# Splitting the first-layer weights of two experts in the second group instead of the first, from pieces loaded a second time

## The chip, the cores and the metric

The kernel runs on one core of one Trainium2 chip. Time is device time in microseconds (us). The kernel before was run three times: 985.46, 986.72 and 987.31, median 986.72. Beside these there is one profiled execution, of 984.69 us; every time that is quoted from a profile is counted from the start of its span, in which the instructions lie (982.9 us).

## What is computed

Two blocks in a row. The first is a recurrent attention over 4 batches, 8 heads, 768 positions and head size 48:

```python
state = alpha[:, :, t, :, None] * state + k[:, :, t] (outer) v[:, :, t]
y[:, :, t] = q[:, :, t] @ state
```

Its output is laid out as x with 3072 rows and 384 columns. The second block adds up four experts, each a pair of matrix products:

```python
p = domain_probs / (domain_probs.sum(-1, keepdims=True) + 1e-09)
for e in range(4):
    h = np.maximum(x @ w1[e], 0.0)          # 384 -> 1024
    out += p[:, e:e + 1] * (h @ w2[e])      # 1024 -> 384
```

All inputs and the output are 32-bit floats.

## The kernel before

The 3072 rows are 24 units of 128 rows, one for each batch and each block of 128 positions. The units stand in seven groups: group 0 has two units, groups 1 to 5 have four, group 6 has two. For each group and expert the kernel runs a first layer, `up` (L922), in eight chunks of 128 hidden columns, and a second layer, `down` (L982), which adds up each unit's 384 output columns over the chunks. The experts are taken in the order 0, 1, 2, 3 in even groups and 3, 2, 1, 0 in odd ones (`expert`, L196), so that the last expert of a group is the first of the next and its weights stay where they are. In group 1 the order is therefore 3, 2, 1, 0. Below, up(1,2) is the first layer of group 1 with the expert at place 2 of its order, which is expert 1.

The attention of a group's units runs beside the layers of the group ahead: `deal` (L1069) lays out by hand-written costs and due times when each step of a unit's attention is put into the program, and `advance` (L1125) puts in what is due after each chunk or step. All engines' queues are in the order in which the program was written (manual_schedule, L1131), and each engine works its queue in that order: PE (TensorE) for the products, ACT (ScalarE) and DVE (VectorE) for everything that reads PSUM and for the attention's elementwise work, POOL (GpSimd) for the stores and some multiplications, SP (SyncE) for the loads.

**Weights.** Group 0 multiplies with the weights as they are (L951 and L1023, tile raw). From group 1 on each weight is used as two parts, a rounded top and the rest, and each product is made of three (`PRODUCTS`, L101). `split_piece` (L240) makes the parts of a piece, a quarter of one expert's layer (128 partitions by 768 numbers): ACT copies the piece into the rounded type (L250), DVE subtracts it from the piece (L252), and POOL stores both parts, 768 KB, to the buffer `kept` in DRAM (L253). `background` (L255) carries the splits on, one step of each open split and one new one per call. In group 0 all four experts' first-layer pieces are split, in group 1 the second-layer pieces (and the last expert's first two of them at the end of group 0).

`load_piece` (L213) loads. A raw piece is 384 KB, from the weights themselves (L232 for the first layer, L236 for the second); a split one is 768 KB from kept (L225). In up(g,e) the next expert's first-layer pieces are loaded at the end of chunks 1, 3, 5 and 7 (L971), into one of four buffers, when PE has read the piece that was there.

**The pool raw** has twelve buffers of one piece each, which are handed out in turn. Raw pieces take them, and from the end of group 1 on the in-order attention (units from the eleventh on) keeps eight for good: two for the loads of q by fours (L184), one zeroed block (L553), one for quads (L611), two for AT and QT (L481), and two for the last group's x (L657).

The rows that the prediction follows, by line: in the attention of a unit, DVE transposes alpha, k and q (L702; L488 in the in-order form); ACT copies half of q (qb, L756) and of k (L774) level by level, and DVE multiplies both with the decays (L763, L775); PE makes the scores (sc L782, far L838), DVE takes them under masks (L792), ACT copies them into lat (L851, L855); PE makes yps (L877) and sps (L904), ACT and DVE turn yps into the two parts of x (L889, L890), DVE updates the state (L909 to L912). In the layers: PE one (L951, L957), ACT relu (hT L953, L959), DVE the rest of hT (L979), PE ops (L1023), and ACT or DVE add ops up into acc (L1047, L1049). ops and one share four PSUM buffers.

Of the kernel before, what the change touches and what calls it, by code (L numbers as in the profile page):

```python
# [20 lines left out]
def kernel(  # L21
# [134 lines left out]
    def load(u, names):  # L156
        if u >= len(units):
            return
        cb, b = units[u]
        for nm in names:  # L160
            src = srcs[nm][b, :, cb * P:(cb + 1) * P, :].rearrange("h s d -> s h d")
            if u == in_fours and nm == "q":
                nc.gpsimd.memset(row_a, 1.0)
            if u == in_runs and nm != "v":
                nc.gpsimd.memset(runs_of[nm][:, :, RUN - HD // 4:], 0.0)
            for g in range(P // QUAD if u >= in_runs and nm != "v" else 0):
                i, tail = divmod(g, 2)
                off, n = (QUAD, RUN - HD // 4) if tail else (0, RUN)
                runs = srcs[nm][b].rearrange("(a i) s d -> i a (s d)", i=2)[
                    i, :, cb * P * D:(cb + 1) * P * D].rearrange("a (t n) -> t a n", t=QUAD)  # L170
                nc.sync.dma_start(out=runs_of[nm][QUAD * g:QUAD * (g + 1), :, :n],
                                  in_=runs[:, :, off:off + n])
            if u >= in_runs and nm == "a":
                continue
            if u < in_fours or nm != "q":
                nc.sync.dma_start(out=raw(u, nm)[:, :, :D], in_=src)
                continue
            by_four = lambda t: t[b, :, cb * P:(cb + 1) * P].rearrange("h (t f) d -> t h (f d)", f=FOUR)
            if u == in_fours:
                four_tiles.extend(whole_raw().rearrange("p (h f d) -> p h f d", f=FOUR, d=D) for _ in range(2))  # L180
            fours[u] = four_tiles
            for i, t in enumerate(fours[u]):
                for j in range(FOUR):
                    nc.sync.dma_start(out=t[j::FOUR].rearrange("p h f d -> p h (f d)"),  # L184
                                      in_=by_four(q)[:, H // 2 * i:H // 2 * (i + 1)])
            for j in range(FOUR - 1):
                nc.sync.dma_start(out=row_a[j::FOUR].rearrange("p h f d -> p h (f d)")[:, :, D * j:],
                                  in_=by_four(alpha)[:, :, D * (j + 1):])
# [13 lines left out]
        return kept[l][expert(gi, e) * NQ + c]  # L202

    AHEAD = 4
    RAW = 3 * NQ

    def parts_of(l):
        return wts.tile([P, 2, KC * QF], F32R, name=f"w{l + 1}", bufs=AHEAD if l == 0 else NQ)
# [4 lines left out]
    def load_piece(l, i, beside=False, held=None):  # L213
        if i >= E * NQ * LAST:
            return
        gi, k = divmod(i, E * NQ)
        at, c = divmod(k, NQ)
        e = expert(gi, at)
        if at == 0 and gi > 0:
            if held is not None:  # L220
                wt[l][i] = held
            return
        if gi > l:
            w = wt[l][i] = parts_of(l)
            nc.sync.dma_start(out=w.bitcast(F32), in_=stored(l, i))  # L225
            return
        if l == 1 and gi == 0 and not beside:
            return
        w = work.tile([P, KC * QF], F32, name="raw", bufs=RAW)
        wt[l][i] = w  # L230
        if l == 0:
            nc.sync.dma_start(  # L232
                out=w.rearrange("p (c f) -> p c f", f=QF),
                in_=moe_w1[e].rearrange("(c p) f -> p c f", p=P)[:, :, c * QF:(c + 1) * QF])
        else:
            nc.sync.dma_start(  # L236
                out=w.rearrange("p (c d) -> p c d", d=DM),
                in_=moe_w2[e].rearrange("(c p) d -> p c d", p=P)[:, c * FPQ:(c + 1) * FPQ])

    def split_piece(l, i):  # L240
        gi, k = divmod(i, E * NQ)
        whole = wt[l][i]
        w = parts_of(l)
        if l == 1:
            wt[l][i] = w
        elif k >= (E - 1) * NQ:
            wt[l][i + NQ] = w
        top, rest = (w[:, part] for part in range(2))

        nc.scalar.copy(out=top, in_=whole)  # L250
        yield
        nc.vector.tensor_sub(rest, whole, top.bitcast(F32))  # L252
        nc.gpsimd.dma_start(out=stored(l, i), in_=w.bitcast(F32))  # L253
# [212 lines left out]
        load(2, "v")  # L466
        yield

    def whole_raw():
        return work.tile([P, KC * QF], F32, name="raw", bufs=RAW)  # L470

    def in_order(u):
        cb, b = units[u]
        k = u - in_fours
# [1 line left out]
        if k < 2:  # L476
            AT_of.append(work.tile([P, NP, P], F32, name="AT"))
            QT_of.append(work.tile([P, NP, P], F32, name="QT"))
        elif k == 2:
            for tiles in (AT_of, QT_of):  # L480
                tiles.append(whole_raw()[:, :NP * P].rearrange("p (a n) -> p a n", n=P))  # L481
        AT, QT = AT_of[k % 3], QT_of[k % 3]
        rv = values[u % 2]

# [65 lines left out]
            next_k(li)  # L550
            yield
        if k == 0:
            fifth = whole_raw()[:, :NP * P].rearrange("p (a i n) -> p a i n", i=2, n=HALF)  # L553
            nc.gpsimd.memset(fifth, 0.0)
            free.append(fifth)
        for li in range(2, 6):
# [51 lines left out]
        if keep:  # L608
            next_k(6)
            if not quads:  # L610
                quads.append(whole_raw()[:, :NP * P])  # L611
# [24 lines left out]
        def tail():  # L636
# [17 lines left out]
            if slot == 0 and gi < LAST:  # L654
                xTs[gi] = work.tile([P, 2, KC, NT], F32R, name="xT", bufs=2)
            elif slot == 0:
                xTs[gi] = [work.tile([P, KC * QF], F32R, name="raw", bufs=RAW) for _ in range(2)]  # L657
# [32 lines left out]
    def attention(u):  # L690
# [172 lines left out]
        def result():  # L863
            yps = ps.tile([P, KC, P], F32, name="yps", tag="w")
            strips = [[] for _ in range(P // QUAD)]
            for c in range(KC):
                for j, strip in enumerate(strips):
                    p, part = divmod(len(strips) * c + j, 3)
                    terms = [(flat_st[:, p, QUAD * part:QUAD * (part + 1)], QT[:, p, :])] if cb > 0 else []
                    for i in range(2):  # L870
                        if part != 2 * (1 - i):
                            at = VD * (2 * p + i) + QUAD * part - D * i
                            terms.append((flat_v[:, at:at + QUAD], lat[:, 2 * p + i, :]))
                    strip += [(c, n == 0, n == len(terms) - 1, *term) for n, term in enumerate(terms)]
            for turn in zip(*strips):
                for j, (c, begins, ends, lhsT, rhs) in enumerate(turn):
                    nc.tensor.matmul(yps[QUAD * j:QUAD * (j + 1), c, :], lhsT=lhsT, rhs=rhs,  # L877
                                     start=begins, stop=ends)
            gi, slot = place[cb, b]
            cols = slice(slot * P, (slot + 1) * P)  # L880
            if gi == 0:
                nc.scalar.copy(out=xTs[gi][:, 0, :, cols], in_=yps)
                return
            if slot == 0 and gi < LAST:
                xTs[gi] = work.tile([P, 2, KC, NT], F32R, name="xT", bufs=2)
            elif slot == 0:
                xTs[gi] = [work.tile([P, KC * QF], F32R, name="raw", bufs=RAW) for _ in range(2)]
            top, low = (x_part(gi, part)[:, :, cols] for part in range(2))
            nc.scalar.copy(out=top, in_=yps)  # L889
            nc.vector.tensor_sub(low, yps, top.bitcast(F32))  # L890
# [31 lines left out]
    def up(gi, e, fc, slots=None):  # L922
# [59 lines left out]
    def down(gi, e, slots):  # L982
# [234 lines left out]
```

## Time and profile before

| | us |
|---|---|
| three runs, median | 986.72 |
| the profiled execution | 984.69 |
| its span | 982.9 |
| PE busy | 960.5 (98%) |
| DVE busy | 602.2 (61%) |
| ACT busy | 382.7 (39%) |
| POOL busy | 107.1 (11%) |
| group 0, from the first product of up(0,0) to the last of down(0,3) | 21.8 to 151.6 |
| group 1: up(1,1), down(1,1) | 194.1 to 214.0, to 235.1 |
| up(1,2), down(1,2) | to 254.3, to 275.4 |
| up(1,3), down(1,3) | to 296.6, to 318.3 |

The clock that PE was granted is full (0.998). The DMA engines moved 188.56 MB, 29.49 MB of it on the queue of POOL, the rest almost all on that of SP.

How to read the views that follow. A line of the timeline has the start and length in us, the engine, the line of the kernel, the operation, what it writes <- what it reads, the shapes and how many instructions were merged; in square brackets stands how long the engine was idle before, and what ended the idle time. SPq lines are SP issuing a DMA, not the transfer. PEld is PE's loading of weights, which runs beside its products.

### The profile page before, as it was taken

To read this page: it belongs to the slowest core of one execution; us is meant where nothing else is said; L and a number is where in the kernel's file an instruction comes from. 1 tells how busy PE (TensorE), PEld (TensorE's weight loads), DVE (VectorE), ACT (ScalarE), POOL (GpSimd) and SP (SyncE) were. 2 spreads that over 40 slices of the span, in tenths; PEclk is the share of its full clock that TensorE was granted. 3 is DMA by queue.
4 is the path that set the end of the run, shared out by engine and by line. 5 is a ranking of instruction groups with operands and counts; after the bars stand their busy time and mean duration, and the time that the engine had idled before them with its cause. 6 is when DMAs were issued, how large, how long until landed. Compare 5 with 4: busy or idle time off the path is not lost.

```text
span 982.9 us, 20423 instructions
## 1 busy us (share of the span) xinstructions
PE 960.5 (98%) x8168; PEld 859.1 (87%) x8168; DVE 602.2 (61%) x1208; ACT 382.7 (39%) x834; POOL 107.1 (11%) x137
## 2 busy tenths in 40 slices
PE   8998899999999999999999999999999999999998
PEld 7776677988989889899899899898898999999997
DVE  4788878576788958668558577568677312222222
ACT  4767655463543542432433423434334122111111
POOL 2000001000212210110210110210120000000000
PEclk9999999999999999999999999999999999999999
DMA  9798977485964877864667884669782006060601
GB/s 196 261 298 223 302 219 253 157 260 170 313 214 141 251 229 224 303 221 114 194 209 238 284 240 117 186 196 270 243 213 78 34 1 257 1 254 3 242 31 33
DMA packets 171490, 188.56 MB, mean 192 GB/s; under 512 B 80588, under 2 KB 151116, under 8 KB 171396
## 3 DMA queue, kind: packets, MB, share of 16 engines
q1 hardware_dynamic: 164932, 157.41, 53.3%
q0 software_dynamic: 6016, 29.49, 7.9%
q8 instruction: 64, 1.05, 0.4%
q10 hardware_dynamic: 448, 0.36, 0.1%
q14 instruction: 30, 0.25, 0.1%
HBM read 154.71 MB, written 32.51 MB: 190 GB/s over the span
## 4 chain that ended last, share of the span: by engine, by line
PE 81%; DVE 9%; ACT 4%; DMA 3%; issue 2%; SPq 0%; DVEq 0%; POOL 0%; ACTq 0%; POOLq 0%
PE ops L1023 38%; PE one L957 31%; PE sc L578 3%; PE yps L650 2%; ACT qb L756 2%; DVE w L252 1%; PE sc L782 1%; DVE hT L979 1%; PE yps L877 1%; PE one L951 1%; DMA raw<-in_moe_w_dram 1%; DVE near L792 1%; DMA w<-kept 1%; PE tp L283 1%; PE far L586 1%
## 5 line engine op out<-in xcount | busy, mean ns | idle before, releaser
L1023 PE MATMUL ops<-w,hT 128*128 128x384 f32 x2112 | 377.9, 338 | 2.4 <-DVE hT L979 2.3
L1023 PEld LDWEIGHTS ops<-w,hT 128*128 128x128 f32 x2112 | 365.2, 188 | 8.2 <-DVE hT L979 4.1
L957 PE MATMUL one<-xT,w 128*128 128x512 f32 x1440 | 333.2, 390 | 0.1
L957 PEld LDWEIGHTS one<-xT,w 128*128 128x128 f32 x1440 | 269.4, 188 | 56.7 <-DVE hT L979 1.0
L959 ACT ACTIVATE hT<-one 128x512 fp32r<-128x512 f32 (+1 forms) x192 | 108.0, 563 | 315.6 <-PE one L957 315.0
L979 DVE SCALAR_TENSOR_TENSOR hT<-one,hT 128x512 fp32r<-128x512 f32 (+1 forms) x192 | 121.0, 641 | 106.7 <-ACT hT L959 106.6
L1049 DVE SCALAR_TENSOR_TENSOR acc<-ops,p_all,acc 128x384 f32<-128x384 f32 x66 | 38.7, 610 | 87.0 <-PE ops L1023 86.9
L756 ACT COPY qb<-QT 64x256 f32<-64x256 f32 x126 | 51.5, 409 | 33.3 <-DVE QT L763 17.9
L531 DVE TENSOR_TENSOR QT<-QT,AT 128x256 f32<-128x256 f32 x70 | 33.1, 472 | 50.4 <-ACT qb L525 40.0
L492 POOL TENSOR_TENSOR ra<-ra 128x384 f32<-128x384 f32 x28 | 28.7, 1026 | 298.8 <-DMA ra<-in_alpha_dram 297.7
L951 PE MATMUL one<-xT,raw 128*128 128x256 f32 (+1 forms) x240 | 44.9, 340 | 0.4 <-ACT xT L453 0.4
L1058 POOL DMA_DIRECT2D out_dram<-acc x22 | 12.0, 548 | 305.3 <-DVE acc L1049 304.4
L1023 PE MATMUL ops<-raw,hT 128*128 128x384 f32 x128 | 44.9, 493 | 0.0
L253 POOL DMA_DIRECT2D kept<-w x32 | 17.2, 539 | 247.6 <-DVE w L252 120.1
L951 PEld LDWEIGHTS one<-xT,raw 128*128 128x128 f32 x240 | 38.0, 191 | 5.2 <-ACT xT L453 0.6
L763 DVE TENSOR_TENSOR QT<-QT,AT 128x256 f32<-128x256 f32 x60 | 25.3, 421 | 26.2 <-ACT qb L756 25.8
L494 POOL TENSOR_TENSOR raw<-raw,ra 128x576 f32<-128x576 f32 x28 | 40.6, 1470 | 1.1
L957 PE MATMUL one<-raw,w 128*128 128x256 f32 x288 | 35.2, 283 | 0.0
L957 PEld LDWEIGHTS one<-raw,w 128*128 128x128 f32 x288 | 35.1, 192 | 0.0
L1023 PEld LDWEIGHTS ops<-raw,hT 128*128 128x128 f32 x128 | 23.1, 190 | 13.4 <-issue 0.6
L525 ACT COPY qb<-QT 64x256 f32<-64x256 f32 x80 | 32.1, 402 | 7.0 <-DVE QT L531 3.5
L792 DVE COPY_PREDICATED near<-masks,sc 128x256 f32<-128x256 uint8 x54 | 28.8, 533 | 7.2 <-PE sc L782 6.2
(163 smaller groups left out, 957.9 us busy)
## 6 DMA issues: line engine op xcount, KB each, us to landing
w<-kept SPq DMA_DIRECT2D x108, 768.0 KB, 6.1
kept<-w POOLq DMA_DIRECT2D x32, 768.0 KB, 6.8
raw<-in_moe_w_dram SPq DMA_DIRECT2D x44, 384.0 KB, 7.1
raw<-in_q_dram SPq DMA_DIRECT2D x112, 96.0 KB, 2.8
rv<-in_v_dram SPq DMA_DIRECT2D x24, 192.0 KB, 3.8
rk<-in_k_dram SPq DMA_DIRECT2D x22, 192.0 KB, 2.9
out_dram<-acc POOLq DMA_DIRECT2D x22, 192.0 KB, 2.3
sa<-in_alpha_dram SPq DMA_DIRECT2D x44, 88.0 KB, 3.7
```

Of the source, the lines that this page charges most:

```text
L494: nc.gpsimd.tensor_mul(t[:, :, 1:], t[:, :, 1:], row_a[:, H // 2 * i:H // 2 * (i + 1)])
L525: nc.scalar.copy(out=qbs[li][rows, :, i, :].rearrange("p a (b r) -> p a b r", r=m), in_=qv[rows])
L531: nc.vector.tensor_mul(qv, qv, spread(dv[:, :, :, 0], m))
L578: nc.tensor.matmul(banks[li // 2 - 1][HALF * s:HALF * (s + 1), li % 2, 2 * p:2 * p + 2, :], lhsT=KTs[li][:, p, HALF * s:HALF * (s + 1)], r ...
L756: nc.scalar.copy(out=qb[rows, :, i, :].rearrange("p a (b r) -> p a b r", r=m), in_=qv[rows])
L792: nc.vector.copy_predicated(near.rearrange("p a (b two r) -> p a b two r", two=2, r=m)[:, :, :, 1, :], mk.unsqueeze(1).broadcast_to([P, H, ...
L951: nc.tensor.matmul(one, lhsT=w[:, kc], rhs=xTs[gi][:, 0, kc, lo:hi], start=(kc == 0), stop=(kc == KC - 1))
L957: nc.tensor.matmul(one, lhsT=w[:, of_w, kc], rhs=x_part(gi, of_x)[:, kc, :n], start=k == 0, stop=k == len(turns) - 1)
L959: nc.scalar.activation(out=parts[0], in_=one, func=ACT.Relu)
L979: nc.vector.scalar_tensor_tensor(out=low, in0=x, scalar=0.0, in1=top.bitcast(F32), op0=ALU.max, op1=ALU.subtract)
L1023: nc.tensor.matmul(sums[slot], lhsT=h, rhs=w, start=(n == begins[slot]), stop=(n == ends[slot]))
L1049: nc.vector.scalar_tensor_tensor(out=acc, in0=part, scalar=scale, in1=acc, op0=ALU.mult, op1=ALU.add)
```

## The change

The first-layer pieces of experts 0 and 1 (places 0 and 1, `LATE = 2`) are not split in group 0 any more. In group 1 those experts stand at places 3 and 2. Where the kernel before loads their two parts from kept in up(1,1) and up(1,2), the changed one loads the raw piece again into the pool raw; and down(1,1) and down(1,2) then hand four splits each to `background`, which in a second layer of group 1 is called at each twelfth of its 96 steps. There each split takes a buffer of w1 and stores its parts to kept as before. The four w1 splits of the first expert at down(0,0) and the four of the second (two in down, two in up(0,1)) are gone. The pool raw becomes twelve tiles with names of their own, that a list hands out in turn; what the attention keeps is taken out of the list.

```diff
-    RAW = 3 * NQ
+    def raw_tile(i, dtype=F32):
+        return work.tile([P, KC * QF], dtype, name=f"raw{i}", bufs=1)
+
+    raws = deque((i, raw_tile(i)) for i in range(3 * NQ))
+
+    def whole_raw(keep=False):
+        if keep:
+            return raws.popleft()[1]
+        raws.rotate(-1)
+        return raws[-1][1]
...
-        if gi > l:
+        late_split = l == 0 and gi == 1 and e < LATE
+        if gi > l and not late_split:
             w = wt[l][i] = parts_of(l)
             nc.sync.dma_start(out=w.bitcast(F32), in_=stored(l, i))
             return
         if l == 1 and gi == 0 and not beside:
             return
-        w = work.tile([P, KC * QF], F32, name="raw", bufs=RAW)
+        w = whole_raw()
...
+    LATE = 2
+
     def split_piece(l, i):
         gi, k = divmod(i, E * NQ)
         whole = wt[l][i]
         w = parts_of(l)
-        if l == 1:
+        if gi == 1:
             wt[l][i] = w
...
-        if gi == 0 and e > 0 and fc in SPLIT_AT:
+        if gi == 0 and e >= LATE and fc in SPLIT_AT:
             making.append(split_piece(0, e * NQ + SPLIT_AT[fc]))
...
-        if gi == 0 and e < E - 1 and slots[0] == (e == 0):
+        if gi == 0 and LATE <= e + 1 < E and slots[0] == (e == 0):
             making.extend(split_piece(0, first + NQ + k) for k in range(2))
...
         while fresh(gi) and (making or splitting):
             background()
+        if gi == 1 and E - LATE <= e + 1 < E:
+            making.extend(split_piece(0, first + NQ + k) for k in range(NQ))
...
-            if n == FCH // 2 and ahead:
-                making.extend(split_piece(0, k) for k in range(NQ))
```

At the places that keep a buffer, `whole_raw()` becomes `whole_raw(keep=True)`, and the last group's x takes `raw_tile(raws.popleft()[0], F32R)`.

More of the change, by code (lines that the diff above doesn't have):

```diff
@@ L179, in load @@
             if u == in_fours:
-                four_tiles.extend(whole_raw().rearrange("p (h f d) -> p h f d", f=FOUR, d=D) for _ in range(2))
+                four_tiles.extend(whole_raw(keep=True).rearrange("p (h f d) -> p h f d", f=FOUR, d=D) for _ in range(2))
             fours[u] = four_tiles
@@ L467, in rest_of_first @@
         yield
-    def whole_raw():
-        return work.tile([P, KC * QF], F32, name="raw", bufs=RAW)
     def in_order(u):
@@ L480, in in_order @@
             for tiles in (AT_of, QT_of):
-                tiles.append(whole_raw()[:, :NP * P].rearrange("p (a n) -> p a n", n=P))
+                tiles.append(whole_raw(keep=True)[:, :NP * P].rearrange("p (a n) -> p a n", n=P))
         AT, QT = AT_of[k % 3], QT_of[k % 3]
@@ L552, in in_order @@
         if k == 0:
-            fifth = whole_raw()[:, :NP * P].rearrange("p (a i n) -> p a i n", i=2, n=HALF)
+            fifth = whole_raw(keep=True)[:, :NP * P].rearrange("p (a i n) -> p a i n", i=2, n=HALF)
             nc.gpsimd.memset(fifth, 0.0)
@@ L610, in in_order @@
             if not quads:
-                quads.append(whole_raw()[:, :NP * P])
+                quads.append(whole_raw(keep=True)[:, :NP * P])
             by_quad = quads[0].rearrange("x (t a c) -> x t a c", a=NP, c=QUAD)
@@ L656, in tail @@
             elif slot == 0:
-                xTs[gi] = [work.tile([P, KC * QF], F32R, name="raw", bufs=RAW) for _ in range(2)]
+                xTs[gi] = [raw_tile(raws.popleft()[0], F32R) for _ in range(2)]
             top, low = (x_part(gi, part)[:, :, cols] for part in range(2))
@@ L886, in result @@
             elif slot == 0:
-                xTs[gi] = [work.tile([P, KC * QF], F32R, name="raw", bufs=RAW) for _ in range(2)]
+                xTs[gi] = [raw_tile(raws.popleft()[0], F32R) for _ in range(2)]
             top, low = (x_part(gi, part)[:, :, cols] for part in range(2))
```

## The prediction, made before the result was known

> **What bounds the kernel now.** I read the page first, then busy times by stage, the chain of waits, and the timelines of the stages that the change touches. Below, up(g,e) and down(g,e) are the first and second layer of group g with the expert at place e of its order; all times are of the one profiled execution. The page:
>
> ```profile
> span 982.9 us, 20423 instructions
> PE 960.5 (98%) x8168; PEld 859.1 (87%) x8168; DVE 602.2 (61%) x1208; ACT 382.7 (39%) x834; POOL 107.1 (11%) x137
> ```
>
> PE (TensorE) is nearly full, so only PE's few waits can be won back, and only new PE waits can lose. The busy times by stage (columns: stretch, its length, then PE, PEld, DVE, ACT, POOL busy, clock, DMA share, GB/s):
>
> ```profile
> 60.00:80.00 20.00, 17.23 (x186) 12.90 (x185) 16.19 (x35) 14.83 (x36) 1.06 (x2) 1.00 1.03 327
> 80.00:100.00 20.00, 18.61 (x185) 14.44 (x183) 18.37 (x39) 12.99 (x32) 1.59 (x3) 1.00 0.81 217
> 214.00:235.00 21.00, 21.00 (x223) 20.45 (x224) 10.87 (x27) 5.81 (x14) 0.00 (x0) 1.00 0.79 262
> 254.00:275.00 21.00, 20.89 (x223) 20.15 (x222) 15.04 (x32) 8.47 (x19) 5.27 (x4) 1.00 0.92 322
> ```
>
> The first two are group 0: PE has holes there, DVE and ACT are the busy pair, and the chain of waits from 47 to 121 us runs over them, not over PE. The last two are down(1,1) and down(1,2), where the splits go: PE is full, DVE and ACT have room. PE's own timeline of group 0 names the holes:
>
> ```profile
> 65.77 0.66 PE L838 MATMUL far<-qb,KT 128*64 128x128 f32 x8 [0.91 <-ACT qb L756]
> 71.79 0.66 PE L283 MATMUL tp<-ident,KT 128*128 128x128 f32 x4 [0.35 <-DVE KT L775]
> 75.24 1.08 PE L877 MATMUL yps<-lat,rv 128*32 128x128 f32 x32 [1.50 <-ACT lat L855]
> ```
>
> Five more follow (0.97, 1.24, 0.75, 1.07, 1.29 us, to 133.75), all on ACT: 8.1 us of PE waits in all. That is the most that group 0 can give.
>
> **What is removed.** Eight splits leave group 0. Each is an ACT copy (L250, median 0.83 us), a DVE subtraction (L252, 0.95 us), and a POOL store of 768 KB (L253, 0.53 us to issue). The instruction order of the built programs puts the removed ones between 36 and 68 us and leaves every other engine order in group 0 as it was.
>
> The first expert's four (36 to 44 us) are worth nothing: PE runs without a hole from 34.62 to 65 us, and DVE then waits for PE anyway (2.37 us for sps at 45.75). The second expert's:
>
> ```profile
> 57.16 2.00 DVE L252 TENSOR_TENSOR w<-raw,w 128x768 fp32r<-128x768 f32 x2
> 61.41 0.98 DVE L252 TENSOR_TENSOR w<-raw,w 128x768 fp32r<-128x768 f32 x1
> 67.84 0.95 DVE L252 TENSOR_TENSOR w<-raw,w 128x768 fp32r<-128x768 f32 x1
> ```
>
> That is 3.93 us of DVE, all on the chain, plus an ACT copy at 53.99 that held the next qb copy (L756) by 0.6. But not all of the 4.5 survives. ACT must pass hT (L953, 59.72) first, which waits for PE's third chunk of up(0,1): PE starts it at 58.12 and needs 1.35, so 59.47. The qb copy behind it moves only from 60.00 to 59.78, and DVE's L763 behind that from 62.31 to 60.65: 1.66 is kept. Going on row by row with the durations of the rows: the AT transpose (L702) 64.87 to 62.85, the QT transpose 68.70 to 65.85 (the last subtraction gone), the qb copy 70.63 to 67.6, the lat copies' end (L855) 75.2 to 72.2. PE, freed of its first two holes, would come to yps at 72.2 as well, in place of 75.24. So **3.0 us** at that point. From there to 135 us the order is as before and the later holes hang on the same engines, so all of it moves by 3.0. Bounds: 4.5 if nothing of ACT's tie to PE holds; 1.3 (the first two holes) if another producer stands at the third.
>
> The stores removed are 6.3 MB. Queue q0 moved 29.49 MB in 7.9% of 982.9 us, so this is some 16.6 us of a DMA that is full (0.96 to 1.03) in that stretch. I count it at nothing, because in the waits from 21 to 146 us no compute engine waits for a DMA.
>
> **What is added.** In up(1,1) and up(1,2), eight loads of 768 KB from kept become eight of 384 KB from the weights; down(1,1) and down(1,2) get four splits each. One is begun at each of steps 12, 24, 36 and 48 of 96.
>
> Down(1,1): four times 0.83 on ACT and 0.95 on DVE go into 21 us in which they are 5.81 and 10.87 busy. The third and fourth ACT copy stand ahead of the xT copy (L889, 225.06). Their pieces are issued on SP at 215.47 or earlier; at the 7.7 to 8.4 us that the w2 pieces took to land there, they are in by 224 at the worst, while ACT sat idle 4.91 us before L889. DVE's last subtraction comes after the takes (L792) and is covered by its 1.61 wait for sps at 231.94. **Nothing.** Without that cover: 1.0.
>
> Down(1,2) is the place that can hurt. SP's queue and the two instructions that matter:
>
> ```profile
> 261.67 0.60 SPq L184 DMA_DIRECT2D raw<-in_q_dram  x1
> 262.37 1.93 SPq L187 DMA_DIRECT2D ra<-in_alpha_dram  x3
> 264.40 1.14 SPq L225 DMA_DIRECT2D w<-kept  x2
> ...
> 263.86 0.48 ACT L889 CAST xT<-yps 128x384 fp32r<-128x384 f32 x1 [4.91 <-PE yps L877]
> 264.37 0.56 DVE L890 TENSOR_TENSOR xT<-yps,xT 128x384 fp32r<-128x384 f32 x1 [1.76 <-ACT xT L889]
> ```
>
> Pieces three and four take the place of the two w<-kept at 264.40, behind the eight L184 and three L187 loads that SP issues from 250.67 on. But ACT's copy of piece three now stands ahead of L889, which was ready at 263.86. So ACT waits for that landing, and behind it L889, DVE's L890, the takes, the accumulations L1049 that free PSUM, and the two subtractions. Two things decide.
>
> When does piece three land? SP's waits there are for the q loads (5.1 us, four times) and for w<-kept (0.9 twice): each load waits for the one eight places before. With half the bytes in pieces one and two ahead of them, I work out some 3 us less, so piece three issues at 261.1. The shortest landing of a w1 piece was 4.2 us, that of the w2 pieces of this stage 6.4; two new stores of 768 KB run beside. I take 4.9, nearer the lower, for the w2 pieces stood behind 1.5 MB and this one does not: 266.0. L889 then starts at 266.85, **3.0 us** late.
>
> What of it reaches PE? The delay plus the two subtractions, less the waits that they fill:
>
> ```profile
> 281.64 0.43 DVE L763 TENSOR_TENSOR QT<-QT,AT 128x256 f32<-128x256 f32 x1 [2.47 <-ACT qb L756]
> ```
>
> Replayed with the rows' durations, the last hT subtraction of up(1,3), which PE waits for at 296.58, comes later by the delay less 2.3 (less 1.5, if DVE's slow rows beside POOL at 268 and 271 only shift). For 3.0 that is 0.7 to 1.5; I take **0.9**. From 297 us PE is full again and keeps what it gets. Bounds: 0 (landing by 265.3) and 5.8 (below).
>
> [...]
>
> **Sum:** -3.0 + 0 + 0.9 = **-2.1 us**. The profiled execution took 984.69 (span 982.9 and 1.8 around it), so 982.6; the median of the three runs is 2.0 higher, 986.72, and against it I predict **984.6**, 0.21% faster. About 0.2% (2.0 us) is what a measurement of this kernel can tell from no change.
>
> **Rivals.**
> *A, slower: ACT held by the third piece in down(1,2).* If SP gains nothing and piece three goes out at 264.40 and takes the 6.4 us of the w2 pieces, it lands at 270.8; L889 is 7.8 late, and the cost 5.8 (the middle of 5.5 and 6.3): net +2.8, **989.5**. The point of no gain is a landing at 268.0; past 270.0 the kernel is slower by over 0.2%. For it: DMA share 0.92 there, two new stores in the same time. Against it: the halved loads ahead, and a DMA nearly empty at 262 to 264 us (112 GB/s). Chance 0.24.
> *B, no gain in group 0.* The wait at 75.24 goes to another producer, 1.3 stays: with 0.9 paid, -0.4, **986.3**. For it: ACT is tied to PE's chunks, as at 59.72. Against it: every hole from 75 on is on ACT, which stands behind the moved work. Chance 0.16.
> *C, more.* The tie at 59.72 costs less, piece three lands in time: -4.0 (between 3.0 and 4.5), **982.7**. Chance 0.10.
> That the splits are not moved at all is excluded by the built order.
>
> **How the numbers follow.** The forecast case has 0.50, net -3.3 to -0.8, its upper end where piece three lands later by 1.3; 0.36 of it is beyond -2.0 and 0.14 within. A: 0.20 slower, 0.04 within. B: 0.12 within, 0.02 to either side. C: 0.10 faster. So faster 0.48, same 0.30, slower 0.22. The range reaches from a net -4.5 with nothing lost (982.2, and 0.4 for the median's scatter: 981.8) up into A, where no more than 2 in 10 is left out: 988.8. The forecast case's own range is 983.4 to 985.9.
>
> **What would show it.** Right: no L250 between 36 and 65 us; the yps of 75.24 some 3 us earlier, PE's waits of 60 to 80 us down from 2.8 to near nothing; down(1,1) still 21 us; in down(1,2) an ACT wait before L889 of some 3 us past yps; up(1,3), 275.4 to 296.6 before, 1 us longer. Wrong: if up(1,3) is 4 us longer or more, A has it; if PE's waits in group 0 stay near 8 us, B; if down(1,1) grows, the cover I counted there was not there. Anything after 320 us that moves by more than a few tenths is a cause that I have not seen.

## The result and the profile after

| | before | after |
|---|---|---|
| runs, median of 9 (lowest to highest), us | 986.58 (983.68 to 988.1) | 990.59 (988.57 to 993.41) |
| ratio, with its 95% interval | | 1.0044 (1.0028 to 1.0061) |
| the profiled execution, its span | 984.69, 982.9 | 991.43, 989.6 |
| granted clock in it, mean | 0.998 | 0.991 |

The change makes the kernel slower by 0.44%. The forecast said 984.6 us, and the time lies above the upper end of the range, 988.8; it is near rival A's 989.5. Of all runs quoted here and below one, of the kernel called group 1 alone, took 1189.72 us at a mean granted clock of 0.753 and is left out. In the changed kernel the lines stand lower in the file: the split's copy, subtraction and store are L262, L264 and L265, the copy of yps and its rest L898 and L899, SP's raw loads L242 and L246, the additions to acc L1058, the layers L960, L966 and L1032. First the head of its page:

```profile
span 989.6 us, 20406 instructions
PE 965.7 (98%) x8168; PEld 864.2 (87%) x8168; DVE 605.2 (61%) x1208; ACT 382.1 (39%) x834; POOL 107.2 (11%) x137
```

PE is busy for 5.2 us more with as many products, so the loss is not waits alone: part of the time products took longer. The busy times by stage (columns as in the prediction; the third row, 275 to 297 us, holds the products of up(1,3), 275.25 to 293.92 in the kernel before, and there the start of down(1,3) too):

```profile
214.00:235.00 21.00, 21.00 (x223) 20.45 (x224) 14.36 (x31) 8.85 (x18) 2.13 (x4) 1.00 0.98 348
254.00:275.00 21.00, 20.89 (x223) 20.14 (x222) 10.67 (x22) 9.26 (x19) 1.06 (x2) 1.00 0.94 314
275.00:297.00 22.00, 17.23 (x97) 13.60 (x96) 21.51 (x38) 8.39 (x15) 7.02 (x8) 0.84 0.57 180
60.00:80.00 20.00, 19.24 (x199) 14.90 (x198) 14.66 (x33) 15.65 (x38) 0.00 (x0) 1.00 0.74 185
```

Last row, group 0: PE is busy for 2.0 us more of the 20. First row, down(1,1): DVE rises from 10.87 to 14.36 and ACT from 5.81 to 8.85, and PE stays full. Second row, down(1,2): PE is still full, but DVE does less than before (10.67, not 15.04): its work is late. Third row: PE lacks 4.8 us, the clock is 0.84, and DVE has no room (21.51 of 22). For the kernel before the same row is

```profile
275.00:297.00 22.00, 20.54 (x123) 16.29 (x122) 19.23 (x35) 11.38 (x22) 2.73 (x5) 1.00 0.65 197
```

**Where the 6.7 us of span come from.** Up(0,0) starts at 22.48 and not at 21.80. These 0.68 are put down to chance and not to the change: when both kernels were profiled again, the start was 22.52 before and 21.38 after. Against that start, yps in group 0 comes 2.28 earlier (73.63 and 75.24). At 119 us the clock falls (0.50 from 119.56 to 122.97) and takes 1.57 back, so at 133.7 us the two kernels are level, and from there to 275 us they can be compared row by row. Down(1,2) and up(1,3) then cost 5.56: the layer behind down(1,3) starts at 323.70, before at 318.14. Down(1,3) itself starts 7.1 us late (301.22, before 294.14), and 1.5 of that come back in it, most of it a wait of PE (1.13 us at 296.58) that is gone. Some 0.5 is won back up to 689 us, where the clock falls once more (0.50 from 689.58 to 692.99), for 1.58.

Timeline rows of the changed kernel for group 0 (PE), and for down(1,2) (SP, POOL, ACT, DVE, PE):

```profile
73.63 1.08 PE L886 MATMUL yps<-lat,rv 128*32 128x128 f32 x32 [0.76 <-ACT lat L864]
...
247.75 3.92 SPq L171 DMA_DIRECT2D sq<-in_q_dram  x4
251.76 9.17 SPq L184 DMA_DIRECT2D raw<-in_q_dram  x8
261.03 2.84 SPq L187 DMA_DIRECT2D ra<-in_alpha_dram  x3
263.97 1.68 SPq L242 DMA_DIRECT2D raw<-in_moe_w_dram  x2
...
259.28 0.53 POOL L265 DMA_DIRECT2D kept<-w  x1 [5.93 <-DVE w L264]
260.76 0.53 POOL L265 DMA_DIRECT2D kept<-w  x1 [0.94 <-DVE w L264]
...
269.61 0.83 ACT L262 CAST w<-raw 128x768 fp32r<-128x768 f32 x1 [9.68 <-DMA raw<-in_moe_w_dram]
270.35 0.47 ACT L898 CAST xT<-yps 128x384 fp32r<-128x384 f32 x1
...
270.85 0.56 DVE L899 TENSOR_TENSOR xT<-yps,xT 128x384 fp32r<-128x384 f32 x1 [8.24 <-ACT xT L898]
...
274.06 1.81 DVE L264 TENSOR_TENSOR w<-raw,w 128x768 fp32r<-128x768 f32 x2
...
280.50 1.56 DVE L772 TENSOR_TENSOR QT<-QT,AT 128x256 f32<-128x256 f32 x1
...
283.63 1.14 DVE L1058 SCALAR_TENSOR_TENSOR acc<-ops,p_all,acc 128x384 f32<-128x384 f32 x2
...
284.30 7.14 PE L966 MATMUL one<-xT,w 128*128 128x512 f32 x18 [4.76 <-DVE acc L1058]
```

The rows of the kernel before that they are held against, beside those in the prediction:

```profile
247.74 2.83 SPq L171 DMA_DIRECT2D sq<-in_q_dram  x4
250.67 11.60 SPq L184 DMA_DIRECT2D raw<-in_q_dram  x8
...
273.60 0.40 DVE L763 TENSOR_TENSOR QT<-QT,AT 128x256 f32<-128x256 f32 x1
...
275.58 1.14 DVE L1049 SCALAR_TENSOR_TENSOR acc<-ops,p_all,acc 128x384 f32<-128x384 f32 x2
...
294.14 1.31 PE L1023 MATMUL ops<-w,hT 128*128 128x384 f32 x6 [0.22 <-DVE hT L979]
296.58 1.32 PE L1023 MATMUL ops<-w,hT 128*128 128x384 f32 x6 [1.13 <-DVE hT L979]
```

Read the changed kernel's rows downwards. SP issues the third piece at 263.97, only 0.43 before the place it had. ACT stands at its copy for 9.68 us, until 269.61. The copy of yps, which needed nothing but PE's yps of 263.8, stands behind it and starts at 270.35, 6.49 late. DVE waits 8.24 for that, and the two accumulations of acc that set PSUM buffers free end at 284.77 and not at 276.72. PE, which needs such a buffer for the next chunk, waits 4.76. Of the eight waits of PE that the prediction listed for group 0, the first two (65.77 and 71.79) are gone, and that of yps is 0.76 and not 1.50.

### The profile page after: what moved, and what is told of

The parts are those of the page before. It is cut to its first block, busy times and chain, and to the rows that moved or that the text cites. A ratio compares the mean times of both kernels' runs of the same rounds, so it can differ in the third digit from the quotient of the medians.

```text
span 989.6 us, 20406 instructions
## 1 busy us (share of the span) xinstructions
PE 965.7 (98%) x8168; PEld 864.2 (87%) x8168; DVE 605.2 (61%) x1208; ACT 382.1 (39%) x834; POOL 107.2 (11%) x137
## 4 chain that ended last, share of the span: by engine, by line
PE 83%; DVE 7%; ACT 4%; DMA 3%; issue 2%; SPq 1%; DVEq 0%; POOL 0%; ACTq 0%; POOLq 0%
PE ops L1032 37%; PE one L966 33%; PE sc L587 3%; PE yps L659 2%; PE one L960 2%; ACT qb L765 2%; PE sc L791 1%; PE yps L886 1%; DVE near L801 1%; DMA sq<-in_q_dram 1%; DMA sa<-in_alpha_dram 1%; DVE w L264 1%; DVE QT L772 1%; PE far L595 1%; PE tp L295 1%
## 5 line engine op out<-in xcount | busy, mean ns | idle before, releaser
L1032 PE MATMUL ops<-w,hT 128*128 128x384 f32 x2112 | 378.8, 338 | 0.8 <-DVE hT L988 0.7
L1032 PEld LDWEIGHTS ops<-w,hT 128*128 128x128 f32 x2112 | 366.9, 189 | 5.7 <-issue 2.5
L966 PE MATMUL one<-xT,w 128*128 128x512 f32 x1440 | 336.0, 393 | 4.8 <-DVE acc L1058 4.8
L966 PEld LDWEIGHTS one<-xT,w 128*128 128x128 f32 x1440 | 271.4, 189 | 62.2 <-DVE acc L1058 5.2
L988 DVE SCALAR_TENSOR_TENSOR hT<-one,hT 128x512 fp32r<-128x512 f32 (+1 forms) x192 | 121.1, 642 | 106.2 <-ACT hT L968 106.2
L1058 DVE SCALAR_TENSOR_TENSOR acc<-ops,p_all,acc 128x384 f32<-128x384 f32 x66 | 38.8, 611 | 81.4 <-PE ops L1032 81.3
L265 POOL DMA_DIRECT2D kept<-w x32 | 17.2, 539 | 266.7 <-DVE QT L772 100.0
L960 PE MATMUL one<-xT,raw 128*128 128x256 f32 (+1 forms) x240 | 44.9, 340 | 0.4 <-ACT xT L465 0.4
L1032 PE MATMUL ops<-raw,hT 128*128 128x384 f32 x128 | 45.0, 493 | 0.0
L960 PEld LDWEIGHTS one<-xT,raw 128*128 128x128 f32 x240 | 38.0, 191 | 5.2 <-ACT xT L465 0.6
L966 PE MATMUL one<-raw,w 128*128 128x256 f32 x288 | 35.2, 283 | 0.0
L966 PEld LDWEIGHTS one<-raw,w 128*128 128x128 f32 x288 | 35.1, 192 | 0.0
L1032 PEld LDWEIGHTS ops<-raw,hT 128*128 128x128 f32 x128 | 23.2, 191 | 13.6 <-issue 0.8
```

The costliest lines, as they stand in the source:

```text
L960: nc.tensor.matmul(one, lhsT=w[:, kc], rhs=xTs[gi][:, 0, kc, lo:hi], start=(kc == 0), stop=(kc == KC - 1))
L966: nc.tensor.matmul(one, lhsT=w[:, of_w, kc], rhs=x_part(gi, of_x)[:, kc, :n], start=k == 0, stop=k == len(turns) - 1)
L988: nc.vector.scalar_tensor_tensor(out=low, in0=x, scalar=0.0, in1=top.bitcast(F32), op0=ALU.max, op1=ALU.subtract)
L1032: nc.tensor.matmul(sums[slot], lhsT=h, rhs=w, start=(n == begins[slot]), stop=(n == ends[slot]))
L1058: nc.vector.scalar_tensor_tensor(out=acc, in0=part, scalar=scale, in1=acc, op0=ALU.mult, op1=ALU.add)
```

## The experiments

**A measure that the clock does not blur.** Beside the times I use one stretch of the profiled execution, from the first product of up(0,0) to the first product behind down(1,3), which holds all that the change moves. In some executions PE's clock falls to 0.50 for 3.41 us in it. Such a fall, where PE is the bound, costs 1.57 us: from PE's wait near 119 us to the wait for far it is 13.15 us without a fall (before) and 14.72 with one (after). Near 35 us it is the same: from the wait there to the wait for yps it is 38.33 us without a fall (loads early, again) and 39.90 with one (removal alone). The last column takes 1.57 off for each fall between 30 and 125 us.

| kernel | median, us | ratio to before (95%) | stretch | falls at, us | stretch less falls |
|---|---|---|---|---|---|
| before | 986.58 | | 296.34 | none | 296.3 |
| before, profiled again | | | 296.29 | none | 296.3 |
| after | 990.59 | 1.0044 (1.0028 to 1.0061) | 301.22 | 119.6 | 299.7 |
| after, profiled again | | | 301.68 | 118.8 | 300.1 |
| removal alone | 984.44 | 0.9969 (0.9948 to 0.9990) | 297.25 | 35.0, 120.3 | 294.1 |
| group 1 alone | 990.17 | 1.0037 (1.0019 to 1.0055) | 302.85 | 35.4 | 301.3 |
| loads early | 984.24 | 0.9972 (0.9955 to 0.9989) | 297.44 | 36.0, 121.4 | 294.3 |
| loads early, again | 984.07 | 0.9987 (0.9971 to 1.0003) | 294.22 | none | 294.2 |
| splits late | 987.37 | 1.0005 (0.9984 to 1.0026) | 299.63 | 33.4, 118.7 | 296.5 |
| two splits behind | 989.00 | 1.0030 (1.0016 to 1.0044) | 298.34 | none | 298.3 |
| stores held | 989.03 | 1.0026 (1.0009 to 1.0042) | 299.93 | 119.3 | 298.4 |
| after, wait filled | 990.33 | 1.0040 (1.0024 to 1.0057) | 302.79 | 35.8, 121.1 | 299.7 |
| loads early, waits filled | 984.08 | 0.9989 (0.9971 to 1.0007) | 294.19 | none | 294.2 |

The falls near 283 us, in the kernels where PE waits there, are left in: for the changed kernel it is shown below that they cost nothing. Each ratio is taken against the kernel before on the same chip in the same hour, with 8 to 12 runs of each kernel and 9 to 35 of before, whose median was 985.70 to 986.58; so rows are compared by their ratio or their stretch rather than by the median. Each stretch is of one profiled execution.

**1 and 2. The two halves apart.** The removal alone, in the kernel before: the split of experts 0 and 1 goes, and their parts are read from the place of experts 2 and 3 in kept. So it leaves out the right weights for two experts; the loads keep their size, and only its time counts.

```diff
-        return kept[l][expert(gi, e) * NQ + c]
+        of = expert(gi, e)
+        return kept[l][(of + 2 if l == 0 and of < 2 else of) * NQ + c]
...
-        if gi == 0 and e > 0 and fc in SPLIT_AT:
+        if gi == 0 and e > 1 and fc in SPLIT_AT:
...
-        if gi == 0 and e < E - 1 and slots[0] == (e == 0):
+        if gi == 0 and 2 <= e + 1 < E and slots[0] == (e == 0):
...
-            if n == FCH // 2 and ahead:
-                making.extend(split_piece(0, k) for k in range(NQ))
```

> The kernel before, without the eight splits of experts 0 and 1 in group 0, and with nothing in their place: from group 1 on those experts use the first-layer parts of experts 2 and 3 (loads of the same size from kept), so that part of the result is not the reference's. Theory (what the change takes out of group 0 is a gain, and group 1 loses more): yps of the second unit some 2.3 us earlier than before, against the same start of up(0,0), and the whole 2.3 us under before, about 984.3. Rival (the gain is undone inside group 0, by the granted clock that fell to 0.51 to 0.64 from 119 to 123 us in the changed kernel): the fall shows here too, and the time is within 0.7 us of before. Prediction on record: 3.0 us under before.

And the changed kernel with the splits of group 0 put back, so that only the loads and splits of group 1 are new:

```diff
-        if gi == 0 and e >= LATE and fc in SPLIT_AT:
+        if gi == 0 and e > 0 and fc in SPLIT_AT:
...
-        if gi == 0 and LATE <= e + 1 < E and slots[0] == (e == 0):
+        if gi == 0 and e < E - 1 and slots[0] == (e == 0):
...
+            if n == FCH // 2 and ahead:
+                making.extend(split_piece(0, k) for k in range(NQ))
```

> The changed kernel with the eight splits of group 0 put back: experts 0 and 1 are split in both groups, the result is the same. Theory: down(1,2) and up(1,3) as in the changed kernel, the whole 5.6 us over before, about 992.2, and some 1 to 2 us over the changed kernel. Rival (the loss is in group 0 or after group 2): within 2 us of before.

The removal gains: 0.9969, and 2.2 us of the stretch. What is added in group 1 costs: 1.0037, and 5.0 us of the stretch. Together that makes +2.7, and the changed kernel has +3.3 to +3.8 in its two profiles; 0.6 to 1.1 of it is not explained. By the times alone the two halves are -0.31% and +0.37% against +0.44% for both, with intervals of some 0.2% to either side of each; they agree with the stretch in sign and are too coarse for the sum. So it is not that the gain was missing; it is smaller than what group 1 costs.

**3. The loads early.** The four raw loads for down(1,2) go out together at the end of chunk 1 of up(1,2), ahead of the loads of k and q, and not one by one at the ends of chunks 1, 3, 5 and 7. All splits stay where the change puts them.

```diff
+            elif gi == 1 and e == 2:
+                wt[0].pop(i)
+                for k in range(NQ if c == 0 else 0):
+                    load_piece(0, i + AHEAD + k)
             elif gi != LAST - 1:
                 load_piece(0, i + AHEAD, held=wt[0].pop(i))
```

> The changed kernel with the four raw loads for down(1,2) all issued at the end of the first chunk pair of up(1,2), ahead of the loads of q by fours; the splits stay at steps 12 to 48. Theory (ACT is held at its copy of the third piece until that piece lands, and everything behind it in ACT's queue with it): the third copy runs at about 260 us, the xT copy starts within 1 us of yps, PE's wait of 4.8 us at the start of up(1,3) and the low clock behind it are gone, up(1,3) ends at 297 to 298 us, and the whole is 2 to 5 us under the changed kernel, 984.3 to 986.6. Rival (the added copies, subtractions and stores themselves are too much for down(1,2) and up(1,3)): up(1,3) still ends 3 us or more later than before, and the whole is over 988.5.

It was run a second time, with another profile:

> The kernel with the four raw loads issued early, once more, beside the two others on the same chip. Theory: 984.2 again, faster than before by 0.2 to 0.3%. Rival: the first measurement was a lucky draw of the clock windows; then 985.5 or more.

The whole loss is gone: 984.24 and 984.07, and a stretch of 294.3 and 294.2, which is that of the removal alone (294.1). So four splits in down(1,2) cost PE nothing if their pieces are there. ACT in the second profile, with a first product 1.25 us earlier than before's:

```profile
256.41 0.84 ACT L262 CAST w<-raw 128x768 fp32r<-128x768 f32 x1
260.31 0.48 ACT L898 CAST xT<-yps 128x384 fp32r<-128x384 f32 x1 [3.07 <-PE yps L886]
```

The third piece's copy runs at 256.41, and ACT then waits for PE, not for a DMA. By the stretch this version is 2.1 us ahead of before and 5.4 ahead of the changed kernel. By the times it is clearly faster than the changed one; against before the first interval excludes 1 and the second just includes it, so there the times alone leave it open.

**4 and 5. The same loads, the copies later.** Splits begun at steps 48 to 84, all behind yps:

```diff
-        if gi == 1 and E - LATE <= e + 1 < E:
-            making.extend(split_piece(0, first + NQ + k) for k in range(NQ))
...
+            if gi == 1 and E - LATE <= e + 1 < E and n == 48:
+                making.extend(split_piece(0, first + NQ + k) for k in range(NQ))
```

> The changed kernel with the splits of down(1,1) and down(1,2) begun at steps 48 to 84 in place of 12 to 48, behind the xT copy in ACT's queue; the loads stay where they are. Theory (the order in ACT's queue, not the time of landing by itself): the xT copy follows yps at once, PE does not wait for the accumulations, and the time is that of the early loads plus at most 1 us for subtractions that now run into up(1,3), 984.5 to 987.5. Rival (added work): over 988.5. A second rival (the landing of the third piece itself, wherever the copy stands): ACT waits as long, only later, and the time is that of the changed kernel.

and only the third and fourth split behind yps, at steps 60 and 72:

```diff
-            making.extend(split_piece(0, first + NQ + k) for k in range(NQ))
+            making.extend(split_piece(0, first + NQ + k) for k in range(NQ // 2))
...
+            if gi == 1 and E - LATE <= e + 1 < E and n == 60:
+                making.extend(split_piece(0, first + NQ + k) for k in range(NQ // 2, NQ))
```

> The changed kernel, with the third and fourth split of down(1,1) and of down(1,2) begun at steps 60 and 72 and not at 36 and 48, so that ACT's copies of them stand behind the copy of yps. Loads and their places in SP's queue are as in the changed kernel. Theory: the loss comes only of ACT standing at the third copy with yps queued behind it. Then the copy of yps starts at some 263.5 us again, the four splits fit into the waits that VectorE has up to 297 us, and the time is near that of the loads early, 984.3. Rival: the late landing costs wherever the copies stand, for VectorE does the two subtractions near 271 us or later anyway; then the time is that of all four splits late, 987.4.

With four splits late the loss shrinks to 2.3 us of the stretch (296.5 against 294.2); the time is 987.37, at before's level, and no better: inside the range expected, but with a remainder of 2.3 where at most 1 was expected. With two of them behind yps I expected all of it back, and got 4.1 us of loss, 989.0. Here the theory, as I had put it, fell. ACT and DVE in that kernel, whose rows at this place are some 2.6 us earlier than before's:

```profile
261.24 0.48 ACT L898 CAST xT<-yps 128x384 fp32r<-128x384 f32 x1 [3.93 <-PE yps L886]
261.75 0.41 ACT L783 COPY KT<-KT 128x256 f32<-128x256 f32 x1
267.01 0.83 ACT L262 CAST w<-raw 128x768 fp32r<-128x768 f32 x1 [4.86 <-DMA raw<-in_moe_w_dram]
267.75 0.81 ACT L765 COPY qb<-QT 64x256 f32<-64x256 f32 x2
...
268.59 0.43 DVE L772 TENSOR_TENSOR QT<-QT,AT 128x256 f32<-128x256 f32 x1 [3.57 <-ACT qb L765]
...
280.33 6.00 PE L966 MATMUL one<-xT,w 128*128 128x512 f32 x18 [3.41 <-DVE acc L1060]
```

The copy of yps is free. But the piece lands no earlier, ACT stands at it again for 4.86, and now the qb copy stands behind: DVE waits 3.57 for that, and PE 3.41 for DVE. So it is not the copy of yps that matters but whatever ACT has next: behind it stand copies of the attention that DVE waits for.

**6. What delays the landing.** The two stores of 768 KB that the first two splits of the place send off at 259.28 and 260.76 are held back, to 273 us:

```diff
         nc.vector.tensor_sub(rest, whole, top.bitcast(F32))
+        for _ in range(3 if gi == 1 and l == 0 and i % NQ < 2 else 0):
+            yield
         nc.gpsimd.dma_start(out=stored(l, i), in_=w.bitcast(F32))
```

> The changed kernel, with the stores of the first two pieces of down(1,1) and of down(1,2) held back for three more calls of the background, some 8 us, so that in down(1,2) they go out near 267 and 270 us, behind the landing of the third piece, and not at 259.3 and 260.8. Theory: the transfers are full from 262 to 270 us in the changed kernel (share 1.0, before 0.42 at 262 to 264) because of these two new stores; without them the third piece lands in some 4.2 us from an issue at 263.5 to 264, near 268 and not at 269.5, and the time is some 1.5 us less than the changed kernel's: 989. Rival: the q loads ahead of it set both the issue and the landing; the third copy starts at 269.6 again and the time is 990.5.

The theory holds in the trace; the times (ratio 1.0026, 1.0044 for the changed kernel) point the same way, but their intervals overlap. Transfers at 262 to 264 and 264 to 266 us, in the changed kernel (DMA share and GB/s are the last two columns):

```profile
262.00:264.00 2.00, 2.00 (x65) 1.74 (x66) 0.61 (x1) 0.00 (x0) 0.00 (x0) 1.00 1.03 351
264.00:266.00 2.00, 2.00 (x64) 1.93 (x60) 0.00 (x0) 0.00 (x0) 0.00 (x0) 1.00 0.99 344
```

in the kernel before, which has no stores there:

```profile
262.00:264.00 2.00, 2.00 (x65) 1.75 (x66) 0.60 (x1) 0.14 (x1) 0.00 (x0) 1.00 0.42 112
```

and with the stores held:

```profile
262.00:264.00 2.00, 2.00 (x74) 1.80 (x68) 0.33 (x1) 0.00 (x0) 0.00 (x0) 1.00 0.72 179
264.00:266.00 2.00, 2.00 (x57) 1.93 (x52) 0.00 (x0) 0.00 (x0) 0.00 (x0) 1.00 0.72 210
```

SP's issue and ACT's copy in the timeline of that kernel:

```profile
263.27 1.97 SPq L242 DMA_DIRECT2D raw<-in_moe_w_dram  x2
...
267.17 0.84 ACT L262 CAST w<-raw 128x768 fp32r<-128x768 f32 x1 [7.54 <-DMA raw<-in_moe_w_dram]
```

From issue to ACT's copy it is now 3.9 us and not 5.6, and the stretch is 1.3 to 1.7 shorter. It is still 4.2 us longer than that of the loads early, which differs from the changed kernel only in the place of the loads. Counted from the issue of the place's first piece, so that the start drops out, the third is issued after 21.6 us (after), 22.4 (after, again), 20.3 (group 1 alone), 20.5 (two splits behind), 22.2 (after, wait filled), and before's load in its place after 22.0. ACT's copy starts after 27.2, 27.8, 26.6, 27.2 and 27.3. An issue up to 2 us earlier made the landing hardly earlier: while the stores run, the full transfer engines (share 0.99 to 1.03) set it. With the stores held it is 21.2 and 25.1; with all splits late, which also keeps stores away until 268 us, the issue is at 19.3, and ACT, which copies it after 24.9, finds it there. What sets the issue between 19.3 and 22.4 was not settled.

**7. Does the low clock of 283 to 290 us cost?** Six idle products in PE's wait of 4.8 us:

```diff
+        if gi == 1 and e == E - 1 and fc == 2:
+            busy = ps.tile([P, DM], F32, name="busy", tag="w")
+            for _ in range(6):
+                nc.tensor.matmul(busy, lhsT=ident, rhs=lat.rearrange("p h n -> p (h n)")[:, :DM], start=True, stop=True)
```

> The changed kernel with six idle matmuls of 128x384 (nobody reads the result) ahead of the third chunk of up(1,3), in PE's wait of 4.8 us, so that the clock does not fall at 284 to 291 us. Theory: VectorE's work behind the late eviction sets the end of that stretch (21.5 of 22 us busy), so the low clock costs nothing and the time stays at 990.6. Rival: the low clock of 284 to 291 us is itself what costs; then the time comes down to 987.5 to 989.

The clock stays at 1.00 there, and nothing is won (990.33, stretch 299.7):

```profile
284.00:291.00 7.00, 5.98 (x32) 4.21 (x32) 6.90 (x12) 3.50 (x7) 0.00 (x0) 1.00 0.33 86
```

DVE, busy 6.90 of 7, sets the pace. The low clock, 0.50 from 283.40 to 290.23 us in the changed kernel, did not come where the wait was filled, and costs nothing by itself.

**8. The other falls of the clock.** Idle products in the two waits near 119 us, on top of the loads early:

```diff
+        busy = ps.tile([P, P], F32, name="busy", tag="w") if u == half + B - 1 else None
...
+            for _ in range((0, 0, 3, 4)[li] if busy is not None else 0):
+                nc.tensor.matmul(busy, lhsT=ident, rhs=ident, start=True, stop=True)
```

> The kernel with the four raw loads issued early, plus idle matmuls of 128x128 (identity times identity into a PSUM tile that nobody reads) before the third and fourth chunk's products of the last unit of the second group's attention: three and four of them, where PE waited 0.75 and 1.07 us near 119 to 121 us. Theory: the clock fall at 119 to 126 us, which the kernels without the first group's splits show and the kernel before does not, comes of PE's short waits standing close together there; with PE kept busy it goes, and the time is some 1.6 us less than with the loads early alone: 982.7. Rival: the clock falls whatever PE does there, or by chance; the fall stays and the time is 984.2.

The profile of that kernel has no fall at 119 us, but the median stays, 984.08: the gain that was expected is not there. Whether the fall belongs to the kernels with the removal, one profile does not tell. The two kernels of this study were therefore profiled once more:

> The kernel before, profiled once more. If the clock fall at 119 to 126 us belongs to the kernels without the first group's splits, PE's granted clock stays at 1.00 there and the waits of 65.8 and 71.8 us are there; if falls come by chance, they show here too, and 34 to 39 us shows which of the two the fall there is (the four trials have it, neither of the first two profiles).

> The changed kernel, profiled once more. The shift of 5.5 us between 275 and 302 us and the wait of 4.8 us on VectorE come again, whatever the clock falls do; the falls of 119 to 126 and 688 to 694 us come again if they belong to the schedule, and not if they come by chance.

The changed kernel again shows the 5.3 us wait on VectorE's acc, and a fall at 119 us, but none at 689 us. The kernel before now has a fall at 686 us, which its first profile lacks. Before (again), two stretches of 3.41 us:

```profile
682.52:685.93 3.41, 1.55 (x15) 0.94 (x12) 3.19 (x10) 1.21 (x3) 0.00 (x0) 1.00 1.00 176
685.93:689.34 3.41, 3.41 (x12) 3.40 (x12) 1.63 (x5) 1.85 (x5) 0.00 (x0) 0.50 0.49 135
```

The changed kernel's two falls, each behind the stretch ahead of it:

```profile
116.14:119.56 3.42, 1.59 (x46) 1.32 (x40) 2.31 (x6) 3.15 (x8) 0.00 (x0) 1.00 0.97 313
119.56:122.97 3.41, 3.41 (x63) 2.76 (x58) 2.46 (x6) 0.05 (x1) 0.53 (x1) 0.50 1.07 329
...
686.17:689.58 3.41, 1.73 (x28) 1.42 (x23) 3.22 (x10) 1.21 (x3) 0.00 (x0) 1.00 0.86 157
689.58:692.99 3.41, 3.41 (x13) 3.41 (x12) 1.94 (x6) 1.85 (x5) 0.00 (x0) 0.50 0.50 130
```

And the same waits near 119 us without a fall, in the kernel before and in the loads early, again:

```profile
116.09:119.50 3.41, 2.66 (x51) 1.75 (x49) 2.28 (x7) 3.30 (x8) 0.53 (x1) 1.00 0.92 246
119.50:122.91 3.41, 2.34 (x75) 2.05 (x73) 3.38 (x8) 1.44 (x4) 0.53 (x1) 1.00 1.09 325
```

```profile
113.45:116.87 3.42, 1.80 (x49) 1.52 (x48) 2.31 (x7) 3.33 (x8) 0.53 (x1) 1.00 0.96 294
116.87:120.28 3.41, 3.23 (x75) 2.69 (x76) 3.34 (x8) 1.01 (x3) 0.53 (x1) 1.00 1.04 256
```

The first number behind the length is PE's busy time. In these rows the three falls stand behind stretches in which PE was busy for 1.55, 1.59 and 1.73 of 3.41 us, and behind 1.80 and more the clock stayed at 1.00. The fall at 119.56 comes after two waits of PE, of 0.76 and 1.07 us (to 117.26 and 119.01); the kernel before has the same two, of 0.75 and 1.07 (to 118.85 and 120.60), without a fall. From up(0,0) on, the falls of the changed kernel's first profile begin at 119.56, 283.40 and 689.58 and last 3.41, 6.83 and 3.41 us; what sets these lengths, no run shows.

PE's busy time alone does not decide. In the loads early, again, PE was busy for 1.61 us of the 3.41 from 114.00 to 117.41, and the clock stayed at 1.00 up to 125 us:

```profile
114.00:117.41 3.41, 1.61 (x48) 1.33 (x46) 2.33 (x6) 3.30 (x8) 0.19 (x1) 1.00 1.02 325
...
116.00:119.41 3.41, 2.36 (x73) 2.10 (x73) 3.35 (x8) 1.39 (x4) 0.53 (x1) 1.00 1.08 302
119.41:125.00 5.59, 5.59 (x29) 4.86 (x30) 1.93 (x4) 2.96 (x7) 0.00 (x0) 1.00 0.98 328
```

What decides, the runs do not show. That falls come and go by execution is shown: the same program, the loads early, has two between 30 and 125 us in one profile and none in the other; near 35 us they stand in profiles with and without the splits of group 0; near 686 us both kernels have one in one profile of two. For 119 us it is argued only. The kernel before has the same two waits there, but none of the three profiles with the splits of group 0 shows the fall, and seven of the nine without them and without idle products there do.

## Why the prediction was wrong, point by point

- **Group 0, -3.0: right in kind, mis-sized, -2.28.** It lies within the bounds (1.3 to 4.5). The tie of ACT to PE's third chunk was there, but I let that chunk end at 59.47, 0.25 earlier; hT started at the old place to 0.01 us (60.41, before 59.72, with 0.68 between the starts), and the qb copy behind it did not move either. The AT transpose came forward by 1.46 and not by the 2.0 of my row-by-row count. The wait that is left at yps is 0.76; the later waits are as long as before.
- **First expert's four splits and the eight stores, 0: nothing speaks against it;** the removal alone gains 2.2, all of it seen at yps. They were not removed one by one.
- **Down(1,1), 0: right.** It still takes 21 us, PE full, with ACT and DVE as busy as counted.
- **Down(1,2), +0.9: this step failed; it cost 5.56.** The delay of the copy of yps was 6.5 and not 3.0, and less of it was absorbed.
  - The issue. The step that broke first is "I work out some 3 us less, so piece three issues at 261.1". The issue came at 263.97. SP did wait less, as counted: between its 15 issues of loads of q and alpha that stand ahead of piece three (from 247.74 on) it stood still for 2.6 us in place of 7.6. But the issues themselves took 13.6 us in place of 9.0, so 0.43 was left. In every profile with raw loads at these places they took 12.5 to 13.6, in those with loads from kept 9.0 to 10.7; why, no run shows.
  - The landing. Taken as 4.9 because "the w2 pieces stood behind 1.5 MB and this one does not", it was 5.56, for this one stood beside 1.5 MB of its own kernel's stores, which I had named and not counted. With the stores held it was at most 3.9; and in the kernel before, a load of twice the size at the same place (264.40) landed in 4.67.
  - The share that reaches PE was the delay less 0.9, not less 2.1. DVE's wait of 2.47 at 281.64 was filled as counted. But its two subtractions put 1.7 on top, and the slow rows beside POOL (busy from 276.79 to 281.77, before from 266.58 to 272.01) did not go, they moved: 280.50 took 1.56, where the same operation took 0.40 before (273.60). So the accumulations were 8.05 late, of which 2.47 was absorbed.
- **Rival A was right** in mechanism (ACT held by the third piece), nearly in size (a delay of 7.8 and a cost of 5.8; measured 6.5 and 5.6) and in time (989.5; 990.59). What I held against it, a DMA nearly empty at 262 to 264 us, was the row of a kernel that did not yet have the stores there: 112 GB/s became 351.
- **After 320 us, "a cause that I have not seen": there was one,** the fall of the clock at 689 us; it came in one of the changed kernel's two profiles, and in one of the kernel before. With the fall at 119 us it makes 3.15 of the 6.7 us by which the two first profiles differ. The medians differ by 4.0, the stretch by 3.3.

## What to carry to other kernels

When work is moved to where engines have room, ask first when its data arrive: on an engine that works in order, one instruction ahead of its data stops everything behind it (here ACT, for 9.68 us), whichever that is, and moving one victim out of its way only names the next. Count the transfers that the moved work itself sends off into the gap that its own loads are to use, and put its loads ahead of the long loads in the queue, which here won back the whole loss. Where profiles of two kernels differ by one or two clock falls, take them out before reading a cause into them.

## What I had not expected of the hardware

Behind two waits of PE of no more than 0.76 and 1.07 us, 0.7 us apart, the clock stood at 0.50 for 3.41 us in the changed kernel (from 119.56), which cost 1.57 us besides; behind the same two waits in the kernel before it stayed at 1.00. One program has such falls in one execution and none in another (spans 985.7 and 980.3 for the loads early, of which two falls make 3.1 and an earlier start of up(0,0) 2.5). Loads that were issued up to 2 us apart, counted from the place's first piece, landed within 1.2 us of each other while the transfer engines were full. And where SP waited 5.0 us less between its loads than in the kernel before, its issues took 4.5 us longer: a wait that is saved on a queue is not yet an earlier issue.
